# Attention followed by a mixture of experts: a fixed place for each expert's first block, and three weight loads issued earlier

## The chip, the cores and the metric

The kernel runs on one core of a Trainium2 chip. The core has five engines with queues of their own: TensorE (PE, matmuls and transposes by matmul; its weight loads are listed as PEld), VectorE (DVE), ScalarE (ACT), GpSimd (POOL) and SyncE (SP, which here issues transfers). Transfers that SP issues go to one hardware queue, the indirect ones that POOL issues to another, and both are carried out by the same 16 DMA engines. The metric is the device time of one launch in microseconds, less being better.

## The reference

Two stages follow each other, everything in float32. The first is causal attention with an additive bias, for 8 batches, 8 heads, 576 tokens and head width 64. The second sends each of the 4608 tokens to one of 8 experts.

```python
scores = scale * q @ k.T;  cum = np.cumsum(np.maximum(s, 0), -1)
scores = where(causal, -1e9, scores + minimum(-(cum_i - cum_j), 0))
attn = exp(scores - max);  attn /= attn.sum() + 1e-9
x = (attn @ v)                      # [8, 576, 512], heads side by side

for each batch b, token s in order:
    fresh = argmax(x[b, s] @ w_gate)
    e = fresh if s == 0 or sigmoid(x[b, s] @ w_local) < 0.5 else prev_e
    out[b, s] = softmax(logits)[e] * (relu(x[b, s] @ w1[e]) @ w2[e])
```

w1 is 512 x 1024 and w2 is 1024 x 512 for each expert, 2 MB each. How many tokens an expert gets is known only once the attention is done.

## The kernel before, in words

The order of the work on each engine is the order of the program; nothing reorders it. Three functions follow each other.

**attention** goes over 32 pairs of heads (4 per batch). For a pair it forms the scores of five query blocks (four of 128 queries, one of 64; lines 165 and 178), adds the bias on VectorE (168, 180), masks on GpSimd (171, 183), takes the exponential on ScalarE (192, 197), turns the weights by matmul with an identity (219) and multiplies with the values (236, 244). It is pipelined by one pair: the turning and the values of pair n-1 lie between the scores of pair n. Every fourth pair a batch of x is complete: it is stored to DRAM (249, 252), and its gate logits are computed from it (264 to 284). SP issues the input loads of a batch (`load_batch`, 105 to 108) at the second pair of the batch before, and the bias of a pair (`load_cum`, 118) two pairs ahead into three buffers. No batch is loaded in the last batch's pairs, so that from pair 30 on nothing but the last store of x remains for SP in this function.

**route** turns the logits into tables. VectorE finds each token's expert, carries experts along the sequence, and makes a one-hot array `hot` of 8 x 40 values per partition (398). Two matmuls count (402, 404). VectorE then computes each token's `rank` among its expert's tokens (410, 411), the number of blocks of 128 that each expert needs (`nblk`, 413 to 416), their running sum `bend` (418), the first slot `base` of each expert (420, 421), the expert `ebi` of each of the 43 blocks (423 to 427), and each token's slot, rank + base (430 to 433). From slots, 80 small matmuls (467), fed by VectorE (458, 462) and GpSimd (465), fill a table that says for each slot which token it holds; VectorE reads it out as `idx_g` (the token to read, 472), `idx_s` (the row to write, 475) and `gate` (471).

**experts** goes over the 43 blocks in the order of the experts, so an expert's blocks lie side by side. For a block `load` has SP read the block's expert from `ebi` into a register and issue w1 and w2 of that expert (500, 505), 4 MB, into a pool `wp` of three buffers; `gather` has GpSimd fetch the block's 128 rows of x by an indirect transfer (513); `turn_x` turns them (522, 524); `layer1` multiplies with w1 in two halves (534, 535), `turn_h` turns the result (543, 544), `layer2` multiplies with w2 (550), scales by the gate (552) and scatters the rows to the output (553). Weights are loaded for every block, also where the block before has the same expert. Loads run two blocks ahead, gathers three.

The pools of attention are given back when that function ends, and route's when it ends. A later tile that lies on a former tile's memory waits for the last use of that one. Before the change, `wp` is made in experts, on the memory that route's tiles had.

Of the kernel before, what the change touches and what calls it, by code (L numbers as in the profile page):

```python
# [9 lines left out]
F32 = mybir.dt.float32  # L10
I32 = mybir.dt.int32
Act = mybir.ActivationFunctionType
Alu = mybir.AluOpType
AX = mybir.AxisListType.X
ET = mybir.EngineType
PSUM = bass.MemoryType.PSUM

P = 128
B, H, S, DH = 8, 8, 576, 64
D = H * DH                  # model width  # L20
E, F = 8, 1024
N = B * S                   # tokens
HP = H // 2                 # head pairs of a batch
NPAIR = B * HP
NF = S // P                 # full query blocks
TS = NF * P                 # first token of the tail block
TL = S - TS                 # its length
NB = NF + 1                 # blocks of a sequence, tail included
NM = B * NB                 # token columns [128 tokens each, tails padded]
DK, FK = D // P, F // P  # L30
NBLK = N // P + E - 1       # most blocks of 128 tokens of one expert that N tokens can need
MASKED = -1e9


@with_exitstack
def kernel(
    ctx: ExitStack,
    tc: tile.TileContext,
    q: bass.AP,         # [B, 128 = (head of pair, d), HP, S]
    k: bass.AP,         # as q  # L40
    vm: bass.AP,        # [B, 128 keys, NF, H, DH]
    vt: bass.AP,        # [B, TL keys, H, DH]
    s: bass.AP,         # [B*H, S]
    w_gate: bass.AP,    # [D, E]
    w_local: bass.AP,   # [D, 1]
    w1: bass.AP,        # [E, 128, DK, F]
    w2: bass.AP,        # [E, 128, FK, D]
    out: bass.AP,       # [N, D]
):
    nc = tc.nc  # L50
    mm, tr = nc.tensor.matmul, nc.tensor.transpose
    cum_d = nc.dram_tensor("cum", (B * H, S), F32, kind="Internal")
    x_d = nc.dram_tensor("x_tokens", (N, D), F32, kind="Internal")

    ctx.enter_context(tc.manual_schedule(engines=None))
    const = ctx.enter_context(tc.tile_pool(name="const", bufs=1))
    ident = const.tile([P, P], F32, name="ident")
    make_identity(nc, ident)
    lg = const.tile([P, NM, E + 1], F32, name="lg")
    nc.vector.memset(lg, 0.0)  # L60

    attention(tc, q, k, vm, vt, s, w_gate, w_local, cum_d, x_d, ident, lg)

    ebi = const.tile([P, NBLK], I32, name="ebi")
    idx_g = const.tile([P, NBLK], I32, name="idx_g")
    idx_s = const.tile([P, NBLK], I32, name="idx_s")
    gate = const.tile([P, NBLK], F32, name="gate")
    route(tc, ident, lg, ebi, idx_g, idx_s, gate)
    experts(tc, w1, w2, out, x_d, ident, ebi, idx_g, idx_s, gate)


@with_exitstack
def attention(ctx, tc, q, k, vm, vt, s, w_gate, w_local, cum_d, x_d, ident, lg):
    """x = softmax(causal(q k^T / sqrt(d) - (cum_i - cum_j))) v, token-major, to x_d; its gate and
    locality logits to lg [128 tokens, (batch, block), E + 1]. cum, a sum of values >= 0, never falls,
    so that the bias of a key that isn't masked is never above 0."""
    nc = tc.nc
# [37 lines left out]
    def load_cum(n):  # L115
        if n < NPAIR:
            cbs[n] = p_cb.tile([P, 2, S], F32, name="cb")
            nc.sync.dma_start(cbs[n], cum_d[2 * n : 2 * n + 2, :].partition_broadcast(P))
# [20 lines left out]

    # cum of a block's own queries, one per partition; tails of a pair's two heads in one column  # L140
    cps = ps_t.tile([P, 512], F32, name="cps", tag="t")
# [64 lines left out]
    def turn(n, t):  # L206
        """The weights of a block with their keys on partitions, four tiles of 128 x 128 at a time."""
        sc = scs[n][t]
        if t < NF:
            src = [(sc[:, h, c * P : (c + 1) * P], P) for h in range(2) for c in range(t + 1)]  # L210
        else:
            src = [(sc[:, c * P : min(c * P + P, S)], min(P, S - c * P)) for c in range(NB)]
        pts[n, t] = []
        for i in range(0, len(src), 4):
            some = src[i : i + 4]
            m = some[0][1]
            ps = ps_t.tile([P, 4, P], F32, name="ptp", tag="t")
            for j, (a, z) in enumerate(some):
                tr(ps[:z, j, :], a, ident)  # L219
            pt = p_pt.tile([P, 4, P], F32, name="pt")  # L220
            nc.scalar.copy(pt[:m, : len(some)], ps[:m, : len(some)])  # L221
            pts[n, t] += [pt[:z, j, :] for j, (a, z) in enumerate(some)]
# [63 lines left out]
    for n in range(NPAIR + 1):  # L286
        b, hp = divmod(n, HP)
        if hp == 1:
            load_batch(b + 1)
        load_cum(n + 2)  # L290
        if hp == HP - 1:
            scale_q(b + 1)
# [21 lines left out]
def route(ctx, tc, ident, lg, ebi, idx_g, idx_s, gate):  # L314
    """Each token's expert and gate, and from them blocks of 128 slots that hold tokens of one expert
    each: the block's expert (ebi), and per slot the token to read (idx_g), the row to write (idx_s,
    beyond the rows for an empty slot) and the gate."""
    nc = tc.nc
# [4 lines left out]
    def t(name, shape, dt=F32):  # L323
        return sb.tile(shape, dt, name=name)
# [3 lines left out]

    # constants
    ones = t("r_ones", [P, P])  # L330
# [19 lines left out]

    # the first greatest logit of each token, the softmax, and whether the token takes a fresh expert
    lge = lg[:, :, :E]
# [14 lines left out]
    nc.vector.tensor_scalar(one_z, lg[:, :, E], -1.0, 1.0, Alu.mult, Alu.add)  # L367
    # 1 / (1 + exp(-z)) < 0.5, in float32, exactly where 1 + (1 - z) > 2
    uv = t("uv", [P, 2, NM])
# [5 lines left out]

    # along each sequence, a token that isn't fresh takes the expert before it
    rows = []
# [11 lines left out]
    for u in range(NB):  # L389
# [4 lines left out]

    # one-hot experts, a token's rank among its expert's, and the experts' blocks
    deep = [P, E, NM]
# [18 lines left out]
    nblk = t("nblk", [P, E])  # L415
    nc.vector.tensor_copy(nblk, nblk_i)
    bend = t("bend", [P, E])
    nc.vector.tensor_tensor_scan(bend, ones[:, :E], nblk, 0.0, op0=Alu.mult, op1=Alu.add)
    base = t("base", [P, E])
    nc.vector.tensor_tensor(base, bend, nblk, op=Alu.subtract)  # L420
    nc.vector.tensor_scalar(base, base, float(P), None, Alu.mult)
    past = t("past", [P, NBLK, E])
    nc.vector.tensor_tensor(past, lane[:, :NBLK].unsqueeze(2).to_broadcast([P, NBLK, E]),
                            bend.unsqueeze(1).to_broadcast([P, NBLK, E]), op=Alu.is_ge)
    eb = t("eb", [P, NBLK])
    nc.vector.tensor_reduce(eb, past, axis=AX, op=Alu.add)
    nc.vector.tensor_scalar(ebi, eb, float(E - 1), None, Alu.min)

    # each token's slot: its block and its place in the block
    nc.vector.tensor_tensor(rank, rank, base.unsqueeze(2).to_broadcast(deep), op=Alu.add)  # L430
    nc.vector.tensor_tensor(rank, rank, hot, op=Alu.mult)
# [8 lines left out]

    # the chosen expert's share of the softmax
    den = t("den", [P, NM])
# [7 lines left out]

    # tokens to slots: table[place, (kind, block)] = sum over tokens of [place] x [block] * (id + 1, gate)
    val = t("val", [P, NM, 2, NBLK])
# [25 lines left out]
@with_exitstack  # L478
def experts(ctx, tc, w1, w2, out, x_d, ident, ebi, idx_g, idx_s, gate):
    """out[token] = gate * relu(x w1[e]) w2[e], one block of 128 slots after the other."""  # L480
    nc = tc.nc
# [4 lines left out]

    wp = pool("wp", 3)
    gp = pool("gp", 4)
# [4 lines left out]
    ps_y = pool("ps_y", 2, space=PSUM)  # L493
    ws, xg, xT, hs, hT = {}, {}, {}, {}, {}
    HB = 512

    def load(i):
        if i >= NBLK:
            return
        e = nc.values_load(ebi[0:1, i : i + 1], engines=[ET.SP], min_val=0, max_val=E - 1,  # L500
                           skip_runtime_bounds_check_because="clamped to the experts when it was counted")
        a = wp.tile([P, DK, F], F32, name="w1b")
        z = wp.tile([P, FK, D], F32, name="w2b")
        for t, src in ((a, w1), (z, w2)):
            nc.sync.dma_start(t.rearrange("p c f -> p (c f)"),
                              src[bass.ds(e, 1)].rearrange("o p c f -> (o p) (c f)"))
        ws[i] = a, z

# [47 lines left out]

    for i in range(2):
        load(i)
    for i in range(3):
# [5 lines left out]
    for i in range(NBLK):  # L565
        load(i + 2)
        gather(i + 3)
        layer1(i + 1, 0)
        turn_h(i)
        turn_x(i + 2)  # L570
        layer1(i + 1, 1)
        layer2(i)
# [35 lines left out]
```

## Time and profile before

| | |
|---|---|
| median of 3 runs | 1272.86 us |
| the three runs | 1268.44, 1272.86, 1300.32 us |
| span of the profiled execution | 1289.8 us |
| the profiled execution's own time | not recorded apart from its span |
| TensorE busy in the span | 1195.5 us (93%) |
| VectorE, ScalarE, GpSimd busy | 464.8, 386.9, 180.3 us |
| mean granted TensorE clock | 0.932 |
| moved by DMA | 259.09 MB, mean 201 GB/s |

The span runs from the first to the last instruction of one execution. Of the three runs only the slowest is longer than the profiled span, so that the profiled execution belongs with that one and not with the median; if it was that run, 1300.32 - 1289.8 = 10.5 us lay around the span. A clock of 1.00 is TensorE's full speed; 0.50 is half of it. The releaser of a wait is the instruction whose end let the waiting one start.

### The profile page before, as it was taken

What the parts mean: (1) busy time and instruction counts of PE and PEld (TensorE: products, weight loads), DVE (VectorE), ACT (ScalarE), POOL (GpSimd) and SP (SyncE); (2) the same over time, 40 slices, a digit from 0 to 9 for tenths busy, and PEclk for the clock granted to TensorE, in tenths of its full rate; (3) what the DMA queues carried; (4) which work ended last, traced back from release to release, by engine and by line L of the source; (5) the groups of instructions that cost most, each with busy time, mean ns of one, the idle gap of its engine ahead of it and who ended that gap; (6) DMA issues with size and microseconds to landing.
All of it is one profiled execution on the core that took longest, in us unless ns stands there. A gap on an engine that the chain in (4) does not pass through costs nothing. (4 is left out here: it accounts for less than half of the span.)

```text
span 1289.8 us, 16119 instructions
## 1 busy us (share of the span) xinstructions
PE 1195.5 (93%) x6028; PEld 743.0 (58%) x6028; DVE 464.8 (36%) x914; ACT 386.9 (30%) x1004; POOL 180.3 (14%) x308
## 2 busy tenths in 40 slices
PE   4999999999999999985699999999999999999996
PEld 1677776777777767774444444454444445444443
DVE  3665746465667576745111111111111111111110
ACT  2554645455566556540011111111111111111110
POOL 1111201011212021102111111111111111111100
PEclk9887978789899999995699999999999999999998
DMA  8114151404223322010988777887887778887750
GB/s 292 49 52 151 38 184 38 166 37 155 67 103 118 128 94 74 1 38 0 378 326 322 312 319 285 308 320 314 323 319 312 293 306 320 315 322 316 312 221 3
DMA packets 38974, 259.09 MB, mean 201 GB/s; under 512 B 10925, under 2 KB 10925, under 8 KB 24816
## 3 DMA queue, kind: packets, MB, share of 16 engines
q1 hardware_dynamic: 29904, 237.30, 47.6%
q0 software_dynamic: 6880, 20.72, 4.1%
q8 instruction: 48, 0.79, 0.2%
q10 hardware_dynamic: 2112, 0.04, 0.1%
q14 instruction: 30, 0.25, 0.1%
HBM read 239.01 MB, written 20.86 MB: 201 GB/s over the span
## 5 line engine op out<-in xcount | busy, mean ns | idle before, releaser
L534 PE MATMUL hp<-w1b,xT 128*128 128x512 f32 x688 | 310.7, 595 | 0.8 <-DVE xT L524 0.8
L550 PE MATMUL yp<-w2b,hT 128*128 128x512 f32 x688 | 302.4, 592 | 0.3 <-ACT hT L544 0.3
L535 ACT ACTIVATE hs<-hp 128x512 f32<-128x512 f32 x86 | 51.4, 598 | 610.7 <-PE hp L534 610.7
L550 PEld LDWEIGHTS yp<-w2b,hT 128*128 128x128 f32 x688 | 130.6, 190 | 164.6 <-issue 164.1
L534 PEld LDWEIGHTS hp<-w1b,xT 128*128 128x128 f32 x688 | 127.9, 191 | 145.5 <-issue 144.3
L552 DVE TENSOR_SCALAR y<-yp,gate 128x512 f32<-128x512 f32 x43 | 32.3, 751 | 401.6 <-PE yp L550 401.6
L192 ACT ACTIVATE sc<-sc,st 128x128 f32<-128x128 f32 (+3 forms) x256 | 141.7, 555 | 100.5 <-DVE st L189 100.3
L236 PE MATMUL po<-vb,pt 128*128 128x64 f32 x1280 | 165.8, 279 | 1.6 <-ACT pt L221 1.6
L236 PEld LDWEIGHTS po<-vb,pt 128*128 128x128 f32 x1280 | 163.2, 202 | 2.3 <-ACT pt L221 2.2
L221 ACT COPY pt<-ptp 128x512 f32<-128x512 f32 (+2 forms) x256 | 116.0, 493 | 129.7 <-PE ptp L219 127.8
L168 DVE SCALAR_TENSOR_TENSOR sc<-cb,cq,ps 128x128 f32<-128x128 f32 (+3 forms) x256 | 125.9, 539 | 56.7 <-PE ps L165 54.0
L165 PE MATMUL ps<-kb,qb 64*128 64x384 f32 (+3 forms) x512 | 123.9, 569 | 2.1 <-DVE sc L168 2.1
L553 POOL DMA_INDIRECT out_dram<-y,idx_s x43 | 43.6, 1015 | 562.7 <-DVE y L552 562.7
L219 PEld LDWEIGHTS ptp<-ident,sc 128*128 128x128 f32 x640 | 77.9, 157 | 66.2 <-issue 55.6
L219 PE MATMUL ptp<-ident,sc 128*128 128x128 f32 x640 | 113.2, 315 | 0.0
L189 DVE TENSOR_REDUCE st<-sc 128x2 f32<-128x256 f32 (+3 forms) x128 | 104.2, 814 | 1.0
L171 POOL TENSOR_SCALAR_AFFINE_SELECT sc<-sc 128x256 f32<-128x256 f32 x128 | 52.1, 407 | 369.2 <-DVE sc L168 287.8
L544 DVE COPY hT<-htp 128x512 f32<-128x512 f32 x43 | 29.7, 692 | 155.2 <-PE htp L543 155.2
L180 DVE SCALAR_TENSOR_TENSOR sct<-cb,cq,ps 64x576 f32<-64x576 f32 x64 | 52.0, 813 | 27.2 <-PE ps L178 26.2
L165 PEld LDWEIGHTS ps<-kb,qb 64*128 64x128 f32 x512 | 46.2, 221 | 17.1 <-issue 7.2
L543 PEld LDWEIGHTS htp<-ident,hs 128*128 128x128 f32 x344 | 40.3, 141 | 22.7 <-issue 22.7
L244 PE MATMUL po<-vb,pt 128*64 128x64 f32 x512 | 21.9, 226 | 30.6 <-DVE xb L238 30.6
(122 smaller groups left out, 770.4 us busy)
## 6 DMA issues: line engine op xcount, KB each, us to landing
w1b<-in_w_dram SPq DMA_DIRECT2D x43, 2048.0 KB, 13.1
w2b<-in_w_dram SPq DMA_DIRECT2D x43, 2048.0 KB, 7.9
cb<-cum SPq DMA_DIRECT2D x32, 576.0 KB, 3.8
qb<-in_q_dram SPq DMA_DIRECT2D x8, 1152.0 KB, 5.8
kb<-in_k_dram SPq DMA_DIRECT2D x8, 1152.0 KB, 8.1
vb<-in_vm_dram SPq DMA_DIRECT2D x8, 1024.0 KB, 10.7
x_tokens<-xb SPq DMA_DIRECT2D x8, 1024.0 KB, 6.1
vl<-in_vt_dram SPq DMA_DIRECT2D x8, 128.0 KB, 10.7
```

What stands on the lines that cost most here:

```text
L165: mm(ps[:, h, :w], lhsT=qb[d, hp, t * P : w], rhs=kb[d, hp, :w], start=True, stop=True)
L168: nc.vector.scalar_tensor_tensor(sc[:, h], cb[:, h, :w], cq[:, c : c + 1], ps[:, h, :w], Alu.subtract, Alu.add)
L171: nc.gpsimd.affine_select(out=diag, in_=diag, compare_op=Alu.is_ge, fill=MASKED, base=0, pattern=[[0, 2], [-1, P]], channel_multiplier=1)
L180: nc.vector.scalar_tensor_tensor(sc[d], cb[d, h], cq[d, c : c + 1], ps[d, :S], Alu.subtract, Alu.add)
L189: nc.vector.tensor_reduce(st[:, 0, 2 * t : 2 * t + 2], sc, axis=AX, op=Alu.max, negate=True)
L192: nc.scalar.activation(sc[:, h], sc[:, h], Act.Exp, bias=st[:, 0, c : c + 1], accum_out=st[:, 1, c : c + 1])
L219: tr(ps[:z, j, :], a, ident)
L221: nc.scalar.copy(pt[:m, : len(some)], ps[:m, : len(some)])
L236: mm(po[:, h, :], lhsT=pt[h * (t + 1) + c], rhs=vb[:, c, 2 * hp + h, :], start=(c == 0), stop=(c == t))
L534: mm(ps, lhsT=xT[i][:, c, :], rhs=ws[i][0][:, c, f], start=(c == 0), stop=(c == DK - 1))
L535: nc.scalar.activation(hs[i][:, f], ps, Act.Relu)
L550: mm(ps, lhsT=h[:, c, :], rhs=ws[i][1][:, c, :], start=(c == 0), stop=(c == FK - 1))
```

## The change

Blocks get a new order. Block i, for i from 0 to 7, is now the first block of expert i, whatever the routing says (an expert with no token would have an empty block there). The up to 35 further blocks (`NX`) follow, expert by expert. So the weights of the first eight blocks are known without `ebi`, which keeps 35 entries for the rest.

With that, the loads of blocks 0 to 2 are issued earlier on SP. Blocks 0 and 1 go into a pool `wp` of two buffers, which is now made before attention's pools and lies beside them; SP issues them at pair 30, behind `load_cum(31)`. Block 2 goes into a pool `wp2` of one buffer, made when attention's pools are given back; SP issues it behind the last store of x. Later blocks use the three buffers in turn as before: blocks 0, 1, 3, 4, 6, ... those of `wp`, blocks 2, 5, 8, ... that of `wp2`. Blocks 3 to 7 are loaded from a fixed address at the usual time, two blocks ahead; from block 8 on SP reads `ebi` as before.

In route the counts change: `nblk` becomes the number of further blocks, at least 0; an expert's `base` is 128 times its number; a token whose rank is 128 or more gets `jump` added, the distance from its expert's first block to its further ones, less one block. The rest of the computation stays. Comments and docstrings were also taken out, which shifts line numbers.

```diff
+    wp = [ctx.enter_context(tc.tile_pool(name="wp", bufs=2, reuse_waits="tile"))]
+    ws = {}
+    def weights(i, e):
+        p = wp[i % 3 // 2]
+        a = p.tile([P, DK, F], F32, name="w1b")
+        z = p.tile([P, FK, D], F32, name="w2b")
+        for t, src in ((a, w1), (z, w2)):
+            nc.sync.dma_start(t.rearrange("p c f -> p (c f)"), src[e].rearrange("o p c f -> (o p) (c f)"))
+        ws[i] = a, z
-    attention(tc, q, k, vm, vt, s, w_gate, w_local, cum_d, x_d, ident, lg)
+    attention(tc, q, k, vm, vt, s, w_gate, w_local, cum_d, x_d, ident, lg,
+              lambda: [weights(i, slice(i, i + 1)) for i in range(2)])
+    wp.append(ctx.enter_context(tc.tile_pool(name="wp2", bufs=1, reuse_waits="tile")))
+    weights(2, slice(2, 3))
...
         load_cum(n + 2)
+        if n == NPAIR - HP + 2:
+            late()
...
+    nc.vector.tensor_scalar(nblk, nblk, -1.0, 0.0, Alu.add, Alu.max)
     bend = t("bend", [P, E])
     nc.vector.tensor_tensor_scan(bend, ones[:, :E], nblk, 0.0, op0=Alu.mult, op1=Alu.add)
     base = t("base", [P, E])
-    nc.vector.tensor_tensor(base, bend, nblk, op=Alu.subtract)
-    nc.vector.tensor_scalar(base, base, float(P), None, Alu.mult)
-    past = t("past", [P, NBLK, E])
+    nc.vector.tensor_scalar(base, eidx, float(P), None, Alu.mult)
+    jump = t("jump", [P, E])
+    nc.vector.tensor_tensor(jump, bend, nblk, op=Alu.subtract)
+    nc.vector.tensor_tensor(jump, jump, eidx, op=Alu.subtract)
+    nc.vector.tensor_scalar(jump, jump, float(E - 1), float(P), Alu.add, Alu.mult)
+    past = t("past", [P, NX, E])
...
-    nc.vector.tensor_tensor(rank, rank, base.unsqueeze(2).to_broadcast(deep), op=Alu.add)
+    far = t("far", deep)
+    nc.vector.scalar_tensor_tensor(far, rank, float(P), jump.unsqueeze(2).to_broadcast(deep), Alu.is_ge, Alu.mult)
+    nc.vector.tensor_tensor(far, far, base.unsqueeze(2).to_broadcast(deep), op=Alu.add)
+    nc.vector.tensor_tensor(rank, rank, far, op=Alu.add)
...
     def load(i):
...
-        e = nc.values_load(ebi[0:1, i : i + 1], engines=[ET.SP], min_val=0, max_val=E - 1,
+        if i < E:
+            weights(i, slice(i, i + 1))
+            return
+        j = i - E
+        e = nc.values_load(ebi[0:1, j : j + 1], engines=[ET.SP], min_val=0, max_val=E - 1,
...
-    for i in range(2):
-        load(i)
     for i in range(3):
         gather(i)
...
     for i in range(NBLK):
-        load(i + 2)
+        if i:
+            load(i + 2)
         gather(i + 3)
```

More of the change, by code (lines that the diff above doesn't have):

```diff
@@ L31 @@
 NBLK = N // P + E - 1
+NX = NBLK - E
 MASKED = -1e9
@@ L60 @@
     nc.vector.memset(lg, 0.0)
-    attention(tc, q, k, vm, vt, s, w_gate, w_local, cum_d, x_d, ident, lg)
-    ebi = const.tile([P, NBLK], I32, name="ebi")
+    wp = [ctx.enter_context(tc.tile_pool(name="wp", bufs=2, reuse_waits="tile"))]
[11 more added lines that the diff above has]
+    weights(2, slice(2, 3))
+    ebi = const.tile([P, NX], I32, name="ebi")
     idx_g = const.tile([P, NBLK], I32, name="idx_g")
@@ L68, with attention @@
     route(tc, ident, lg, ebi, idx_g, idx_s, gate)
-    experts(tc, w1, w2, out, x_d, ident, ebi, idx_g, idx_s, gate)
+    experts(tc, weights, ws, out, x_d, ident, ebi, idx_g, idx_s, gate)
 @with_exitstack
-def attention(ctx, tc, q, k, vm, vt, s, w_gate, w_local, cum_d, x_d, ident, lg):
+def attention(ctx, tc, q, k, vm, vt, s, w_gate, w_local, cum_d, x_d, ident, lg, late):
     nc = tc.nc
@@ L419, in route @@
     base = t("base", [P, E])
-    nc.vector.tensor_tensor(base, bend, nblk, op=Alu.subtract)
-    nc.vector.tensor_scalar(base, base, float(P), None, Alu.mult)
-    past = t("past", [P, NBLK, E])
-    nc.vector.tensor_tensor(past, lane[:, :NBLK].unsqueeze(2).to_broadcast([P, NBLK, E]),
-                            bend.unsqueeze(1).to_broadcast([P, NBLK, E]), op=Alu.is_ge)
-    eb = t("eb", [P, NBLK])
+    nc.vector.tensor_scalar(base, eidx, float(P), None, Alu.mult)
[4 more added lines that the diff above has]
+    past = t("past", [P, NX, E])
+    nc.vector.tensor_tensor(past, lane[:, :NX].unsqueeze(2).to_broadcast([P, NX, E]),
+                            bend.unsqueeze(1).to_broadcast([P, NX, E]), op=Alu.is_ge)
+    eb = t("eb", [P, NX])
     nc.vector.tensor_reduce(eb, past, axis=AX, op=Alu.add)
     nc.vector.tensor_scalar(ebi, eb, float(E - 1), None, Alu.min)
-    nc.vector.tensor_tensor(rank, rank, base.unsqueeze(2).to_broadcast(deep), op=Alu.add)
+    far = t("far", deep)
+    nc.vector.scalar_tensor_tensor(far, rank, float(P), jump.unsqueeze(2).to_broadcast(deep), Alu.is_ge, Alu.mult)
+    nc.vector.tensor_tensor(far, far, base.unsqueeze(2).to_broadcast(deep), op=Alu.add)
+    nc.vector.tensor_tensor(rank, rank, far, op=Alu.add)
     nc.vector.tensor_tensor(rank, rank, hot, op=Alu.mult)
@@ L478, in experts @@
 @with_exitstack
-def experts(ctx, tc, w1, w2, out, x_d, ident, ebi, idx_g, idx_s, gate):
+def experts(ctx, tc, weights, ws, out, x_d, ident, ebi, idx_g, idx_s, gate):
     nc = tc.nc
@@ L485, in pool @@
         return ctx.enter_context(tc.tile_pool(name=name, bufs=bufs, reuse_waits="tile", **kw))
-    wp = pool("wp", 3)
     gp = pool("gp", 4)
@@ L493, in experts @@
     ps_y = pool("ps_y", 2, space=PSUM)
-    ws, xg, xT, hs, hT = {}, {}, {}, {}, {}
+    xg, xT, hs, hT = {}, {}, {}, {}
     HB = 512
@@ L499, in load @@
             return
-        e = nc.values_load(ebi[0:1, i : i + 1], engines=[ET.SP], min_val=0, max_val=E - 1,
-                           skip_runtime_bounds_check_because="clamped to the experts when it was counted")
[L502 to L507, printed above, removed]
+        if i < E:
[3 more added lines that the diff above has]
+        e = nc.values_load(ebi[0:1, j : j + 1], engines=[ET.SP], min_val=0, max_val=E - 1,
+                           skip_runtime_bounds_check_because="clamped to the experts when it was counted")
+        weights(i, bass.ds(e, 1))
     def gather(i):
```

## The prediction

> **What bounds the kernel now.** I read the slices of the page first, to see where TensorE is not busy. Each digit is a fortieth of the span, 32.2 us.
>
> ```profile
> PE   4999999999999999985699999999999999999996
> PEclk9887978789899999995699999999999999999998
> DMA  8114151404223322010988777887887778887750
> ```
>
> TensorE is busy everywhere but at the start and in slices 18 to 20, about 575 to 645 us: that is route and the way into the experts. Behind it, it is busy without a gap at full clock while the DMA engines are 70 to 80% busy. The groups of instructions say the same of the experts:
>
> ```profile
> L534 PE MATMUL hp<-w1b,xT 128*128 128x512 f32 x688 | 310.7, 595 | 0.8 <-DVE xT L524 0.8
> L550 PE MATMUL yp<-w2b,hT 128*128 128x512 f32 x688 | 302.4, 592 | 0.3 <-ACT hT L544 0.3
> ```
>
> In all 43 blocks layer 1 waited 0.8 us and layer 2 0.3 us, and neither ever for weights (w1b, w2b). So no weight load is late now, and the change can only move the way into the experts. There the waits of the window 560 to 660 us and the timeline matter. The timeline's columns are start, duration, engine and operation, with the idle time before it in brackets.
>
> ```profile
> PE xp L522 <- DMA xg<-x_tokens,idx_g: 10.0, 1, 10.0
> ```
>
> ```profile
> 614.78 0.37 SPq L505 DMA_DIRECT2D w1b<-in_w_dram  x1
> 615.34 0.95 SPq L505 DMA_DIRECT2D w2b<-in_w_dram  x1
> ...
> 619.52 0.18 DVE L472 TENSOR_SCALAR idx_g<-id 128x43 int32<-128x43 f32 x1
> ...
> 620.67 1.18 POOL L513 DMA_INDIRECT xg<-x_tokens,idx_g  x1 [5.19 <-issue]
> ...
> 629.22 1.08 PE L522 MATMUL xp<-ident,xg 128*128 128x128 f32 x4 [9.98 <-DMA xg<-x_tokens,idx_g]
> 630.34 0.69 DVE L524 COPY xT<-xp 128x512 f32<-128x512 f32 x1 [10.31 <-PE xp L522]
> 631.09 5.12 PE L534 MATMUL hp<-w1b,xT 128*128 128x512 f32 x8 [0.78 <-DVE xT L524]
> ```
>
> The wait that ends last before the first expert is the **gather of x**, not the weights: w1 of block 0, issued at 614.78, landed 7.6 us later, at 622.4, and lay ready when xT came at 631.03. The gather was issued at 620.67 and landed 8.4 us later, at 629.1. Weights count here only as its neighbours: in 620 to 630 us the DMA engines were busy throughout, at 428 GB/s, with the six loads of blocks 0 to 2.
>
> **The change part by part.**
>
> *The three loads leave the gather's window.* What does the same gather take alone? The transfers from POOL, issue to landing, in the windows 620 to 621.5 us and 1258 to 1259 us:
>
> ```profile
> xg<-x_tokens,idx_g POOLq DMA_INDIRECT x1, 8.4
> ```
>
> ```profile
> out_dram<-y,idx_s POOLq DMA_INDIRECT x1, 2.6
> ```
>
> The second is the scatter of block 40, when the last weights had landed; scatters between loads take 8.3 us in the median. Counting the reference's routing gives 41 used blocks, the last with 50 rows; the two scatters behind it write no row and took 2.3 and 2.1 us. So I put the lone gather at 2.6 us plus the other 78 rows of 2 KB, 160 KB at 429 GB/s, 0.4 us: 3.0 us. The bounds are 2.1 us (a transfer of nothing) and 8.4 us (the neighbours did not matter). Gain: 8.4 - 3.0 = **5.4 us**, bounds 6.3 and 0. It is all on the path, since TensorE, VectorE and ScalarE do nothing in these 10 us. What is late next? Not w1: it will have landed long before. Gathers 1 to 3 follow 1.26 us apart, each with block time ahead of it. So xT sets the start again, by its gather.
>
> *A rule against this.* The Trainium skill, "DMA: Bandwidth & Descriptors", section "Queues, rings and completion order", says that each DMA engine takes turns between the queues that have work, packet by packet. By that the weights would cost the gather at most its half share of the rate; with that page's fixed 2.0 us for a transfer from GpSimd ("Anatomy of one DMA"), an estimate from the page is 3.2 us beside weights and 2.6 alone, and the change would lose 0.9 us with the VectorE work below. The 8.4 us measured beside weights is against it, so I keep the rows.
>
> *Route's extra VectorE work.* One instruction on 8 values is added to nblk; base and jump are four where base was two: three more in all, which start 0.20 us apart in this stretch (L418 to L421): +0.6. L423 and L426 shrink from 344 to 280 values: they take 0.51 each, a 320-value one 0.49, so about -0.15 for both. Two operations on 320 values are added for `far`; the nearest row, L430, starts 0.52 before the next: +1.0. Sum **+1.5 us**, bounds 1.2 and 1.9. No other engine works here: TensorE waits 12.64 us for GpSimd's val, which waits for VectorE's blk, so all of it is on the path.
>
> *Loads 0 and 1 at pair 30.* SP issues four more transfers right behind `load_cum(31)`, which in the trace went out at 510.60; SP has nothing else until the last store of x at 567.93. 8 MB at 429 GB/s take 20 us, so they run to about 533 us, in pairs 29 and 30, and the stores at 568 find the queue empty. Queued ahead of them are only the store of batch 6 and cb of pair 31, needed a pair later. What do writes of weights do to the engines? From 631 us on matmuls run with the DMA at full load, 16 in 7.03 us, as later. In attention, pair intervals (between the L201 of one pair and the next, at clock 1.00) are 13.73 to 13.75 us where little is loaded, and 14.46 us just behind a slice with 54% DMA share: 0 to 0.7 us per pair, 0 to 1.4 in all. I take 0.
>
> *Load 2, and where route's tiles lie.* Load 2 waits for the last users of attention's memory (L276, 576.3 us); behind it in SP are only loads that wait for layer 1 of block 0. It lands by about 590, thirty us before the gather. Route's tiles now lie 96 KB further up, on other attention tiles. GpSimd's constants, made at 557.4 to 558.9, could be held until those are free: 0 to 1.6 us if held to 576.3, as VectorE needs them at 576.56. I take 0, for the instruction order has its first constant wait for an old input load and for GpSimd itself, not for the end of attention. The gather's buffers lie on route's tiles; the last of these is read by idx_s, done at 620.03, before 620.67: 0, at most 0.4.
>
> *The blocks.* 43 blocks and 86 loads of 2 MB as before, with the same two-block lead. A block takes 15.05 us (1226.90 to 1241.95 between two L552), its 4 MB land well within that, and TensorE does not wait. Eight register reads fewer on SP are hidden by the two blocks of lead. The tail ends in two empty blocks as now. Worth 0.
>
> *Sum.* -5.4 + 1.5 = **-3.9 us**: in the profiled execution a span of 1289.8 - 3.9 = 1285.9. That execution is slow against the median of the runs; the median becomes 1272.86 - 3.9 = **1269.0 us**. The unknowns together reach from -5.1 to +5.3.
>
> **The clock as the larger unknown.** The three runs differ by 32 us. In the trace the 31 intervals between the pairs' L201 sum to 528.2 us; if all 24 plain ones took 13.74, as the full-clock ones do, and all 7 with logits the shortest, 20.35, it would be 472.2. So 56 us of this execution are half-clock stretches, which begin with the small logits matmuls and end at varying times (granted clock 0.70 to 0.96 in 20 us windows). The change adds no TensorE instruction there, so I give it no sign, but its median can fall elsewhere among such runs. At the start of the experts the clock is 0.50 until about 634 us, and the first eight matmuls took 5.12 us where eight take 3.60 later: +-1.5 us if that moves.
>
> **The rivals.**
>
> *Gather at its own pace* (slower): its 8.4 us is its own, for 128 scattered reads, not its neighbours'. For it: no gather in the trace ran alone; its fastest is 8.4. Against: scatters fall from 8.3 to 2.6. Place: 620.67 to 629.1. Then only the VectorE work remains, +1.5: 1274.4 us. It decides once the gather lands more than 6.9 us after its issue.
>
> *Prefetch in the way*: pairs 29 and 30 stretch by 1.4 us and the constants are held for 1.6: 1269.0 + 3.0 = 1272.0, no change.
>
> *The prefetch does not happen at pair 30*: SP holds it to the end of attention. Then 12 MB start at 576 and are in by 606, still ahead of the gather at 622: again 1269.0. Earliness within attention is worth nothing here.
>
> *Another draw of the clock*: the same change on a median run as long as the slowest shown, 1300.32 - 3.9 = 1296.4, or with 10 us less of half clock, 1259.
>
> **How the numbers follow.** The forecast (own range 1266 to 1272) and the late prefetch with the same time 0.56; gather at its own pace 0.13; prefetch in the way 0.08; another clock draw 0.23, of which 0.15 upwards. The range goes from 1262 (1268.44 less 5.1, rounded down) to 1288, half way between the median and the slowest run, 1286.6, plus the 1.5 of the slower rival. About 2% is what a measurement of this kernel can tell from no change: under 1247.4 us 0.04, over 1298.3 us 0.07, both by the clock alone, and 0.89 between.
>
> **What would show it.** Right: six loads issued before 580 us; the first gather lands about 3 us after its issue; L522 waits some 6 us for it instead of 9.98; GpSimd's first val starts 1.5 us later after the last logits; layer 1 and 2 still wait about 1 us in all; a block still 15.05 us. Wrong: a gather of 7 us or more with the DMA idle around it; L534 or L550 waiting for w1b or w2b; pair intervals at full clock above 14.5 us around 511 to 535; or half-clock stretches whose sum moves by more than the 4 us at stake.

## The result, and the profile after

The changed kernel took 1307.40 us in the median of 5 runs (1297.08 to 1307.67), the kernel before 1297.54 us over its now 5 runs (1268.44 to 1311.90). The ratio of the comparison is 1.0295, 95% interval 1.0226 to 1.0364: slower. This ratio, like every ratio below, leaves out the runs more than 1.5% above a kernel's fastest, here three of the five of before (1297.54, 1300.32, 1311.90) and none of the changed kernel's, while the medians of all five differ by 0.8%.

The lines of the changed kernel that answer to those shown of before. First the slices of its page, then its two matmul groups.

```profile
PE   3999999999999999993899999999999999999996
PEclk9887879788899989995699999999999999999998
DMA  8104141415133231713168887777878777888750
...
L559 PE MATMUL hp<-w1b,xT 128*128 128x512 f32 x688 | 311.3, 596 | 0.8 <-DVE xT L549 0.8
L575 PE MATMUL yp<-w2b,hT 128*128 128x512 f32 x688 | 302.4, 592 | 0.3 <-ACT hT L569 0.3
```

The gap of TensorE in front of the experts (the 19th and 20th slice) is shorter, and the weights of the first three blocks stand as DMA load in the 17th and 19th slice instead of the 20th. The profiled execution took 1297.08 us, 1.7 us more than its span. In every later run, too, the time is 1.7 to 2.0 us above the span, so that the profiled execution of before, with its span of 1289.8 us, took about 1291.7 us: it is none of the three runs listed for it. The experts are as before: 0.8 and 0.3 us of waiting in 43 blocks, 15.05 us a block. The way into the experts, from the timeline (start, duration, engine and operation, idle time before it):

```profile
518.52 0.44 SPq L72 DMA_DIRECT2D w1b<-in_w_dram  x1
519.01 0.42 SPq L72 DMA_DIRECT2D w2b<-in_w_dram  x1
519.48 0.65 SPq L72 DMA_DIRECT2D w1b<-in_w_dram  x1
520.18 0.45 SPq L72 DMA_DIRECT2D w2b<-in_w_dram  x1
...
584.88 0.20 DVE L299 COPY lg<-lps 128x36 f32<-128x36 f32 x1 [9.73 <-PE lps L292]
584.90 0.33 SPq L72 DMA_DIRECT2D w1b<-in_w_dram  x1
...
629.34 0.19 DVE L499 TENSOR_SCALAR idx_g<-id 128x43 int32<-128x43 f32 x1
...
630.49 1.18 POOL L538 DMA_INDIRECT xg<-x_tokens,idx_g  x1 [5.19 <-issue]
...
634.22 1.09 PE L547 MATMUL xp<-ident,xg 128*128 128x128 f32 x4 [5.16 <-DMA xg<-x_tokens,idx_g]
635.35 0.69 DVE L549 COPY xT<-xp 128x512 f32<-128x512 f32 x1 [5.49 <-PE xp L547]
636.09 5.67 PE L559 MATMUL hp<-w1b,xT 128*128 128x512 f32 x8 [0.78 <-DVE xT L549]
```

Loads 0 and 1 went out at pair 30's place, load 2 at 584.90, after the last logits. The gather had the DMA engines to itself: 3.73 us from its issue to the first transposes, where it was 8.55. So the mechanism did what was forecast, and yet the time rose. Cutting both spans at the same instructions shows where. In the kernel before, the instruction that starts "route" is this one:

```profile
576.37 0.20 DVE L283 COPY lg<-lps 128x36 f32<-128x36 f32 x1 [7.04 <-PE lps L276]
```

"Pairs" is from the first to the last L201 (L217 after), "last logits" from there to L283 (L299), "route" from there to idx_g, "gather" from idx_g to the first transposes, "experts" from there to the end; all in us, worked out from the starts in the timelines.

| kernel | start | pairs | last logits | route | gather | experts | span |
|---|---|---|---|---|---|---|---|
| before | 32.4 | 528.2 | 15.8 | 43.15 | 9.70 | 660.6 | 1289.8 |
| changed | 32.2 | 534.2 | 18.5 | 44.46 | 4.88 | 661.2 | 1295.4 |

Route and gather together fell by 3.5 us, from 52.85 to 49.34. Pairs and last logits rose by 8.7 us, and in them the engines' instructions are the same. The intervals of the pairs take the same few values in both traces (13.74 to 15.3, 16 to 18, 20 to 26 with logits) and meet the long ones at other places: the half-clock stretches lie differently. This is what the experiments had to settle: does the change lengthen them, or do they fall so without it?

### The profile page after: what moved, and what is told of

The parts are those of the page before. It is cut to its first block, busy times and chain, and to the rows that moved or that the text cites. A ratio compares the mean times of both kernels' runs of the same rounds, so it can differ in the third digit from the quotient of the medians.

```text
span 1295.4 us, 16086 instructions
## 1 busy us (share of the span) xinstructions
PE 1202.3 (93%) x6028; PEld 749.2 (58%) x6028; DVE 466.0 (36%) x919; ACT 386.9 (30%) x1004; POOL 180.2 (14%) x308
## 6 DMA issues: line engine op xcount, KB each, us to landing
vl<-in_vt_dram SPq DMA_DIRECT2D x8, 128.0 KB, 10.8
```

## The experiments

### The two kernels again, and two halves of the change

Four kernels on one chip, sharing 35 runs of the kernel before.

The changed kernel once more:

> The changed kernel once more, beside new runs of the one before. Theory A (the change is worth -3.5 us, as the two traces show from the last logits to the first expert matmul, and the rest is how long the half-clock stretches of attention happen to last): times spread over the same 1268 to 1312 us that the kernel before has shown, the medians within 10 us of each other in either order. Theory B (something in the change lengthens the half-clock stretches of attention, each time): 1297 to 1308 again, with the kernel before lower by 10 us or more in most runs.

The kernel before, against itself:

> The kernel before against itself. Both theories: a ratio of 1.00, and the spread that no change gives. Theory A needs this spread to reach from about 1268 to 1312 us, so that a ratio of 1.03 can come out of no change at all; theory B needs it to stay mostly below 1300.

The new order without the early loads:

```diff
-    wp = [...tile_pool(name="wp", bufs=2...)]        # ahead of attention
-    attention(..., lambda: [weights(i, slice(i, i + 1)) for i in range(2)])
-    wp.append(...tile_pool(name="wp2", bufs=1...));  weights(2, slice(2, 3))
+    attention(..., lambda: None)
...                                                   # in experts
+    wp = pool("wp", 3)
+    for i in range(2):
+        load(i)
```

> The new block order and route as in the changed kernel, but three weight buffers in experts and the first loads at their old place. Stage by stage: route 1.3 to 1.5 us longer than before (43.2 to 44.6 us from the last logits to idx_g), and the first gather again 8.4 us with loads beside it, so that the first transposes wait about 10 us: +1.5 us in all against before. Rival on the gather (its pace is its own): under 5 us here too. In the total, theory A: anywhere in 1268 to 1312; theory B by the early loads or by the moved memory of attention: as the kernel before; theory B by route: 1307.

The kernel before with attention's memory moved by 64 KB:

```diff
+    loc = ExitStack()
+    spare = loc.enter_context(tc.tile_pool(name="spare", bufs=1))
+    pad = spare.tile([P, 1], F32, name="pad");  nc.vector.memset(pad, 0.0)
+    room = spare.tile([P, 16384 - 1], F32, name="room");  nc.vector.memset(room[:, :1], 0.0)
     attention(...)
+    loc.close()
```

> The kernel before with 64 KB per partition left unused ahead of attention's pools, so that attention lies where it lies in the changed kernel; nothing else differs but two one-column memsets at the start. Theory A: 1268 to 1312, no pattern. Theory B by the moved memory: 1297 to 1308 in nearly all runs. Theory B by the early loads: as the kernel before.

| kernel | median (lowest to highest), runs | ratio to before, 95% interval | pairs | route | gather |
|---|---|---|---|---|---|
| before, shared | 1282.24 (1263.80 to 1315.43), 35 | | | | |
| changed, again | 1285.33 (1260.11 to 1297.15), 12 | 0.9963, 0.9893 to 1.0033 | 502.1 | 44.49 | 4.90 |
| before, again | 1281.14 (1268.37 to 1312.55), 12 | 1.0005, 0.9953 to 1.0058 | 515.5 | 43.17 | 9.82 |
| order only | 1294.49 (1272.85 to 1311.90), 12 | 0.9991, 0.9926 to 1.0056 | 506.8 | 44.48 | 9.92 |
| memory moved | 1278.24 (1268.39 to 1303.80), 12 | 0.9999, 0.9948 to 1.0050 | 513.5 | 43.16 | 9.03 |

The 3% did not come back: the same changed kernel is now level with before, and the unchanged one alone reaches from 1268 to 1313 us. One profile of each kernel is too few to compare the pairs directly, but the clock records of the traces settle it. I added up, in each profile with logits in a row, the time at half clock within the pairs (the time ahead of a trace's first record, at most 10.4 us, counted as half clock): 113.5 us before, 126.3 changed, and 85.3, 57.0, 67.4 and 82.0 us in the profiles of before again, changed again, order only and memory moved, with 88.8 in one more of the changed kernel below. The pairs of all seven are 475.6 us + 0.464 times that time, to 0.3 us. So, to 0.3 us, neither the early loads nor the moved memory lengthens the pairs at a given clock. What differs is how long the clock was at a half. The runs show no lengthening by that way either: the 18 later runs of the changed kernel (the six below included) average 1283.4 us, the 80 later ones of before 1284.8.

What is steady from profile to profile is the rest: route 43.15 to 43.17 us with the old order and 44.46 to 44.49 with the new (+1.3 us), and the gather's 9 to 10 us wherever loads run beside it, 4.9 without them. The gather of "order only" is the old one, with the loads beside it:

```profile
601.30 1.18 POOL L532 DMA_INDIRECT xg<-x_tokens,idx_g  x1 [5.19 <-issue]
610.07 1.09 PE L541 MATMUL xp<-ident,xg 128*128 128x128 f32 x4 [10.19 <-DMA xg<-x_tokens,idx_g]
```

### The logits spread, to take the clock out of the comparison

The pairs vary by 32 us, and the change is worth 3.5. If the half clock begins with the logits matmuls that stand in a row after every fourth pair, spreading them over the next pairs should take most of that away. Each of the five blocks is turned in one step of a pair and projected in the next:

```diff
-        last = turned(0)
-        for t in range(NB):
-            this, last = last, turned(t + 1) if t + 1 < NB else None
-            project(t, this)
+        def piece(t):
+            if t < NB:
+                got[t] = turned(t)
+            if t:
+                project(t - 1, got.pop(t - 1))
...
+        return [lambda t=t: piece(t) for t in range(NB + 1)]
...                                    # in the steps of a pair, behind values()
+            if todo:
+                todo.pop(0)()
...
-            logits(b - 1)
+            todo += logits(b - 1)
```

Done to the kernel before:

> The kernel before with the logits of a batch of x spread over the next pairs of heads: one block's turning and the projection of the block before in each step of a pair, instead of all five blocks in a row, with two buffers of their own for the turned x. The same instructions otherwise. If the half-clock stretches begin because 6.6 us of logits matmuls stand in a row, they go, all pairs take 13.7 to 15.5 us, and the 36 to 62 us that the profiled runs so far spent above full clock (31 intervals summing to 502 to 534 us instead of 472) go with them: 1225 to 1250 us, within 5 us of each other. Rival: the clock drops by small matmuls wherever they stand: 1264 to 1315 again.

to the changed kernel:

> The changed kernel with the logits spread in the same way. If the change is worth -3.5 us and nothing else (from the last logits to the first transposes of x 49.4 us instead of 52.9), 3 to 4 us below the same edit of the kernel before, and the ratio between the two 0.997, now that the clock no longer hides it. If the change itself lengthens half-clock stretches, above it.

to the new order with the loads at their old place:

> New order and route, first loads at their old place, logits spread: 1.3 to 1.5 us above the kernel before with its logits spread, if route's extra VectorE work lies on the path and the gather beside the loads again takes 8.4 us or more. Under 0.5 us apart if that work is hidden.

and to the changed kernel with loads 0 and 1 behind the last store of x:

> The changed kernel with the logits spread, and loads 0 and 1 issued by SP behind the last store of x instead of at pair 30; their buffers are as in the changed kernel. 12 MB from about the end of attention take some 28 us, well before the gather: the same time as the changed kernel with its logits spread, within 1 us, if what counts is only that no load runs beside the gather. If loads in pairs 29 and 30 slow attention: 0.5 to 1.5 us less. If the early issue is worth something itself: more.

| kernel, logits spread | median (lowest to highest) of 6 | ratio to before, 95% interval | pairs | route | gather |
|---|---|---|---|---|---|
| before | 1249.94 (1244.81 to 1257.71) | 0.9830, 0.9762 to 0.9898 | 480.2 | 43.17 | 9.79 |
| changed | 1245.59 (1242.33 to 1251.52) | 0.9796, 0.9728 to 0.9864 | 485.9 | 44.48 | 4.86 |
| new order, old loads | 1249.46 (1244.02 to 1259.54) | 0.9837, 0.9752 to 0.9922 | 477.9 | 44.49 | 9.78 |
| changed, loads 0 and 1 late | 1245.21 (1237.28 to 1256.22) | 0.9776, 0.9693 to 0.9858 | 483.4 | 44.48 | 4.82 |

The 11 shared runs of before had a median of 1280.46 us. Spreading the logits takes about 2% off whatever the order, and narrows the spread from 40 us to some 10 to 20, not to the 5 that I had expected: half-clock stretches still occur, as the granted clock in the slices of the kernel before with its logits spread shows (tenths of full speed; the two 5 are route):

```profile
PEclk9889999998899999955999999999999999999999
```

The profiled runs before this edit had 30 to 62 us above full clock (502.1 to 534.2 less 472), not 36 to 62. Part of the gain is not the clock: at full clock a pair with logits and the one behind it took 20.36 + 14.45 us and now 18.37 + 14.47, so seven batches give 14 us, by filling waits. The pairs of the seven profiles with logits in a row average 516.7 us, of the seven with logits spread 483.2 (the three further kernels below counted); the other 20 us of the 33.5 are less time at half clock. The clock records agree: with logits spread the half-clock time in the pairs averages 44.4 us instead of 88.6, and the seven pairs are 463.1 us + 0.454 times that time, to 0.2 us, so that 12.5 us of the fall are in the constant and 21 in the clock.

With this edit the totals lean the way the traces say. Changed against before: -4.35 us in the medians, -3.7 in the means of six runs (1246.4 against 1250.1); the traces say 52.96 - 49.34 = -3.6. New order with old loads: +0.8 in the means (1250.9), +1.3 in the traces, so the VectorE work of route does lie on the path. Loads issued late: -0.4 in the medians, nothing against this spread; in the traces the gather is the same (4.82 against 4.86), and the pairs, with the half-clock time taken out as above, agree to 0.2 us. So the early issue within attention is worth nothing that shows; that no load runs beside the gather is everything. None of these totals differs from its neighbour by more than the runs of one kernel do; the figures to trust are those of the stages. In the profiles so far route repeats to 0.03 us, and the time from the issue of the gather to the first transposes is 3.67 to 3.75 us alone and 8.55 to 8.77 beside loads.

### What the gather's extra time is

Beside the loads the gather takes 8.4 to 8.6 us from issue to landing, alone 3.5 to 3.6. I had forecast that it would fall, but not why the neighbours cost it 4.8 us. Taking turns between the two queues packet by packet would explain it if packets differ in size. The trace has both queues in the window 620 to 640 us of the kernel before (all packets first, then for each queue its packets, MB and share of the 16 engines):

```profile
DMA packets 841, 8.54 MB, mean 427 GB/s; under 512 B 128, under 2 KB 128, under 8 KB 384
q1 hardware_dynamic: 521, 7.49, 88.4%
q0 software_dynamic: 320, 1.05, 13.0%
```

Leaving out the 64 tiny packets in each queue (under 512 B, 128 in all), a weight packet carries 16 KB and a gather packet 4 KB. So the weights were put into SBUF in shorter pieces, with a gap behind each, in the kernel with new order, old loads and spread logits:

```diff
-        a = wp.tile([P, DK, F], F32, name="w1b")
-        z = wp.tile([P, FK, D], F32, name="w2b")
+        a = wp.tile([P, DK * F // n, n + 8], F32, name="w1b")     # n = 1024: 4 KB; n = 512: 2 KB
+        z = wp.tile([P, FK * D // n, n + 8], F32, name="w2b")
...
-            nc.sync.dma_start(t.rearrange("p c f -> p (c f)"), src[e].rearrange(...))
+            nc.sync.dma_start(t[:, :, :n], src[e].rearrange(...).rearrange("p (g n) -> p g n", n=n))
```

> As order_inter (new order and route, first loads at their old place beside the gather, logits spread), but the weight tiles in SBUF have 32 bytes of gap behind every 4 KB, so that a partition's 16 KB go in four pieces. Beside 16 KB pieces the gather took 8.4 to 8.5 us, alone 3.6 to 3.7: 4.8 us more. If the DMA engines take turns between POOL's and SP's queue piece by piece, the extra time goes with the size of the neighbour's piece: about 1.2 us for a quarter, 4.8 us from issue to landing, while the load rate stays near 429 GB/s. If it is the shared rate or the memory that slows the gather: 8.4 as before.

> The same with a gap behind every 2 KB, eight pieces per partition and load: 0.6 us more than alone, 4.2 us from issue to landing, if turns are taken piece by piece; 8.4 if not. Two things could spoil it: short pieces that are carried together again (then 4.8 as with 4 KB), or a load rate that falls so far that a block of 15.05 us waits for its 4 MB.

The two queues in 20 us around the gathers, with pieces of 4 KB and then of 2 KB:

```profile
q1 hardware_dynamic: 1818, 7.25, 89.2%
q0 software_dynamic: 320, 1.05, 12.9%
```

```profile
q1 hardware_dynamic: 3425, 6.92, 91.4%
q0 software_dynamic: 320, 1.05, 13.1%
```

The weight packets did shrink, to 4.0 and 2.0 KB. The first gather, issue to landing, with 4 KB, with 2 KB and, for comparison, alone in the changed kernel:

```profile
xg<-x_tokens,idx_g POOLq DMA_INDIRECT x1, 6.9
```

```profile
xg<-x_tokens,idx_g POOLq DMA_INDIRECT x1, 6.3
```

```profile
xg<-x_tokens,idx_g POOLq DMA_INDIRECT x1, 3.6
```

Neither expectation holds by itself. Of the 4.8 us, 1.6 go with a quarter of the piece and 2.2 with an eighth; by turns I had forecast 3.6 and 4.2, by the shared rate 0. All 43 gathers of each run say the same way: their median from issue to landing falls from 10.8 us to 7.3 and 6.9. The load rate in the eight microseconds from the gather on hardly moved (433 GB/s with 16 KB, 418, 401).

My forecast by turns was mis-sized, for it let the whole 4.8 us go with the piece. An estimate from the lines above: four gathers make 256 packets, so one makes 64, four on each of the 16 engines if they are spread evenly. By the shares a weight packet occupies an engine for 0.62 us with 16 KB, 0.16 with 4 KB and 0.09 with 2 KB. If each of the four gather packets waits for one weight packet, that is 2.5, 0.6 and 0.3 us, a fall of 1.8 and 2.1 us, near the 1.6 and 2.2 measured. So turns between packets can account for about 2.5 us beside 16 KB pieces. About as much remains at every size (2.4, 2.7 and 2.4 us above the lone gather), and its cause is open. The loads were still in time: the two matmul groups waited 0.8 and 0.3 us with both sizes, while w2's landing went from 7.9 to 9.4 and 9.6 us in the median. The times, 1249.72 and 1245.57 us in the median of two runs each, say nothing among runs that differ by 10.

### The changed kernel a third time

> The changed kernel a third time, unchanged, on whatever chip this call gets. If the first comparison (1.03) was a matter of which clock patterns its five runs met, the ratio is 0.99 to 1.00 again and the profile shows 49.3 to 49.5 us from the last logits to the first transposes; if the change has a slow case of its own, runs at 1307 with the kernel before at 1270 to 1285 beside them.

1295.36 us in the median of 6 runs (1264.15 to 1300.30), beside 1289.51 for before (1262.27 to 1307.34, 11 runs); ratio 1.0018, interval 0.9858 to 1.0179. Route took 44.48 us, the gather 4.83. So of 23 runs of the changed kernel only four of the first five reached 1307 us; the others stay at or under 1300.30.

### A version that fills TensorE's idle stretches

The last run looks for what the clock follows, and for a faster kernel, on the changed kernel with its logits spread:

```diff
+    for _ in range(11):                                   # in route, before the table
+        mm(tot, lhsT=ones, rhs=flat, start=True, stop=True)
     val = t("val", [P, NM, 2, NBLK])
...
+    busy = ps_h.tile([P, HB], F32, name="hp")             # in experts, before the first transposes
+    for _ in range(3):
+        mm(busy, lhsT=ident, rhs=ws[0][0][:, 0, :HB], start=True, stop=True)
     turn_x(0)
```

> The changed kernel with the logits spread and, in TensorE's idle stretches of route, matmuls whose results nothing reads: 11 of 320 columns between the counting matmuls and the table, 3 of 512 columns between the table and the first transposes. The half clock of route (0.50 from the logits on, the table's 80 matmuls taking 17.75 us) comes of TensorE's idleness, by the theory that the clock follows how densely it works: then the clock rises before the table, the table takes 9 to 13 us, the first layer starts at full clock, and the kernel comes out 5 to 10 us below the changed kernel with its logits spread (1245.6 us), near 1237. Rival: the table's own small matmuls pull the clock down again at once: table 17.75 us, gain 0 to 2 us. Against both: if the added matmuls stay at half clock they end up to 1 us after the table's inputs are there.

1243.76 us in the median of 6 runs (1237.43 to 1252.80), ratio to before 0.9758, interval 0.9690 to 0.9827. Its stages of time (busy time of PE, PEld, DVE, ACT and POOL with the instructions in brackets, then granted clock, DMA share and GB/s) around the added matmuls and the start of the table:

```profile
540.00:550.00 10.00, 7.93 (x25) 5.19 (x26) 6.99 (x23) 0.00 (x0) 0.00 (x0) 0.70 0.36 154
550.00:556.00 6.00, 1.78 (x7) 0.95 (x5) 5.69 (x15) 0.00 (x0) 0.00 (x0) 1.00 0.00 0
556.00:560.00 4.00, 1.31 (x6) 1.31 (x7) 2.02 (x2) 0.00 (x0) 3.97 (x4) 0.54 0.00 0
560.00:565.00 5.00, 5.00 (x26) 5.00 (x25) 1.65 (x2) 0.00 (x0) 0.90 (x3) 0.50 0.00 0
```

```profile
545.16 6.62 PE L493 MATMUL tot<-hot,r_ones 128*128 128x320 f32 x22 [0.44 <-DVE rank L442]
558.69 17.76 PE L509 MATMUL table<-val,place 128*128 128x86 f32 x80 [6.91 <-POOL val L507]
576.24 4.75 PE L601 MATMUL hp<-w1b,ident 128*128 128x512 f32 x6
...
582.91 3.67 PE L574 MATMUL hp<-w1b,xT 128*128 128x512 f32 x8 [0.88 <-DVE xT L564]
```

The clock reads 1.00 from 546.1 us, 0.9 us after the first of the added matmuls, to 556.3 us, 4.5 us into the 6.91 us for which TensorE then waits; without them, in the changed kernel with its logits spread, it stays at 0.50 there (532.1 to 586.7 us). In the table it stays at 0.50 for 17.76 us although TensorE counts as busy throughout. So the table gains nothing, as the rival said. The three matmuls ahead of the first layer did what they should: 3.67 us for its first eight matmuls, where the profiles at half clock have 5.1 to 6.8, and it shows as 658.8 us of experts instead of 660.6. The 5 to 10 us of the theory did not come; 1.83 us lie between the medians, 1243.76 and 1245.59, the size of those 1.8 us, but within the runs' spread, and the two were measured on different chips. Both versions with spread logits and early loads beat both kernels.

## Why the prediction was right or wrong

**The sign and the time: not met, and the step that failed is the last one, the clock.** "The median becomes 1272.86 - 3.9" took the centre of three runs as the kernel's time and set the range around it by 1268.44 and 1286.6. The kernel before, run 35 times on one chip, has a median of 1282.24 us and reaches from 1263.80 to 1315.43; the profiled span of 1289.8 had already been a sign that 1272.86 lay low. The term was seen (56 us lost to half clock in the profile) and its size was not: a range by it would have been some 1260 to 1315. (Its lower end was also off in the sum: 1268.44 - 5.1 is 1263.3, not 1262.) The rival "another draw of the clock" (1296.4 upward, 0.15 of the chance) is what the first five runs met, and 11 us more: their mean granted clocks were 0.925, 0.919, 0.919, 0.915 and 0.919, and two later runs of the kernel before at 0.919 took 1308.69 and 1305.61 us. At one clock the two kernels are level to some 3 us; what the five had was a low clock. The reading that half-clock stretches begin with the small logits matmuls is half right: in the profile it came from, 6 of the 13 stretches in the pairs do.

That those runs came out 3% slower is not an effect of the change that any other run shows. Four of the five lie within 0.6 us of each other (1307.12 to 1307.67), and when it was run again, its first three runs lie within 0.3 us (1265.56 to 1265.84) before the spread sets in. So runs that follow each other may be alike, and five of them need not be five draws. That they repeat one pattern is not shown: only one run of each set left a trace, and the clocks of the four differ (0.915 against 0.919). What sets the clock's pattern in a run was not tested and is open.

**The gather.** Forecast 8.4 to 3.0 us, -5.4. Measured 8.4 to 3.6, -4.8. The mechanism is shown, by "order only" (9.92 us with the loads beside it) and by the late loads (4.82 without). The lone gather was mis-sized by 0.6 us: I added the bytes of 78 rows to a scatter of 50, and a gather of 128 rows takes that much more.

**The rule weighed against it.** I read the Trainium skill, "DMA: Bandwidth & Descriptors", "Queues, rings and completion order", as giving the gather half of each engine. The page says turns go packet by packet. If its packets are those that the trace counts, then with 16 KB against 4 KB the gather's turn is a fifth of the time, not half. The two runs with shorter pieces agree with such turns for 1.6 and 2.2 us of the 4.8. They leave 2.7 us that turns do not explain. Dropping the rule for the row was right in the sum and wrong in the reason.

**Route's VectorE work.** Forecast +1.5, measured +1.3 in every profile (43.15 to 43.17 against 44.46 to 44.49).

**Loads 0 and 1 at pair 30.** Forecast 0. In the changed kernel the DMA was full from 523 to 539 us. Two stretches at full clock, the first beside the loads and the second behind them (busy time of PE, PEld, DVE, ACT and POOL, then clock, DMA share, GB/s):

```profile
529.00:539.00 10.00, 9.03 (x83) 6.97 (x84) 7.19 (x13) 6.64 (x20) 1.13 (x4) 1.00 1.01 429
539.00:553.00 14.00, 13.03 (x113) 9.79 (x111) 10.97 (x24) 9.43 (x27) 2.10 (x6) 1.00 0.18 75
```

In both TensorE is idle for 0.97 us, the one wait that every pair has, and for nothing else; the loads cost it nothing. The 14.46 us that I had laid to loads comes behind pairs with logits whether loads run or not: it stands in the kernels with the logits spread too (14.47).

**Load 2, route's tiles, the blocks.** Load 2 went out at 584.90, held to the last logits as forecast, and landed about 12 us later, 33 us ahead of the gather. GpSimd's constants ran at 563.23, 3.17 us ahead of the last L217, as before the change (557.42, 3.17 us ahead of the last L201), and held nobody. Blocks 15.05 us, layer waits 0.8 and 0.3. All as forecast.

**"Earliness within attention is worth nothing."** Shown by the late loads as far as the runs can tell: 1245.21 against 1245.59, the gather 4.82 against 4.86.

**The slower rival** (the gather at its own pace, +1.5) is excluded by 3.6 us. **The rival of a collision** in pairs 29 and 30 is excluded by the stretch above and by the pairs, which at a given clock are the same in all seven profiles to 0.3 us.

## What to carry to other kernels

Before a load is moved earlier, look which wait ends last where it is used: here the weights had long been there, and the gain of 4.8 us came only from taking 12 MB off the DMA engines while a small gather was due. Where the spread between runs is ten times the change, a total cannot judge it; stages cut at the same instructions in two traces can, to some 0.1 us, and a stage whose length follows the clock can be judged once its half-clock time is taken out (here to 0.3 us of 500). The cause of the spread is worth more than the change (2% here, against 0.3%). A range for the time has to take in that spread, and three runs do not show it.

## What the runs showed of the hardware that I had not expected

- A gather of 256 KB beside loads at 429 GB/s takes 8.4 to 8.6 us instead of 3.6, and part of that, about 2 us, goes with the size of the pieces in which the loads are written (6.9 us at 4 KB, 6.3 at 2 KB).
- TensorE's clock does not follow its busy share as the profile counts it: 80 matmuls of 86 columns kept it "busy" for 17.75 us at a clock of 0.50 throughout, while with 22 matmul instructions of 320 columns, 6.62 us, it rose to 1.00 within their first 0.9 us, and it fell to 0.50 again 4.5 us into a wait.
- In a loop in which TensorE is about 94% busy, 29 of the 49 rows of small matmuls (9 columns) in the seven profiles had a half-clock stretch beginning in them or within 1 us behind; 55 of the 84 stretches begin elsewhere, most of them 10 to 38 us behind the end of another. None lasted longer than 13.7 us. Spreading the small matmuls left 48 stretches in seven profiles and shortened the 31 intervals by 33.5 us on average, about 20 of it by the clock.
- How long the pairs take follows from the time at half clock alone, to 0.3 us, in seven profiles of four kernels that reach from 502 to 534 us: each microsecond at half clock costs 0.46 us.
